# Block attention fused with two feed-forward layers: attention's small products in four quarters of the TensorE array, and the first block begun in another order

## The chip, the cores and the metric

One core of one Trainium2 chip runs the whole kernel. The metric is the device time of one execution in microseconds (us); lower is better. The kernel before took 1273.2 us (median of three runs).

## What is computed

Attention within chunks of 64 tokens (8 batches, 8 heads, 576 tokens, head size 64), then two feed-forward layers over the 4608 tokens of width 512. All data are float32.

```
scores = scale * q_c @ k_c^T ; scores -= max(scores) ; attn = exp(scores)
attn = attn / (sum(attn) + 1e-9) ; out = attn @ v_c        # per chunk of 64 tokens and head
h = x @ w_in ; g = h * clip(h + 3, 0, 6) / 6 ; y = g @ w_out            # 512 -> 2048 -> 512
h = y @ w_in2 ; solu = h * softmax(h) ; ln = layernorm(solu) * g_ln ; out = ln @ w_out2   # 512 -> 1024 -> 512
```

## The kernel before, in words

**Units and blocks.** Attention is done in 36 units. A unit holds two chunks of 64 tokens for all 8 heads, one chunk on partitions 0 to 63 and the other on 64 to 127. Four units make a block of 512 tokens, and the first layer runs over nine blocks (`b` from 0). A block is 16 steps `f`: `moe_h(f)` is 12 matmuls of 128x512 (line 376), ScalarE and VectorE make the gate from its result (lines 382, 386) and split it in a rounded high part and a low rest (393, 396), and `moe_o(f)` is 12 matmuls into four accumulator banks (407). `moe_o` runs one step behind `moe_h`.

**Attention beside the blocks.** While block `b` is multiplied, the attention of block `b+1` is worked off in `slot(b, f)` (line 800), one unit per group of four steps. At the end of a group the slot issues the product with v of one unit (`attn_pv`, line 355) and then the scores of the next (`scores`, line 279). In the steps between come the exponentials, the normalisation (`attn_norm`) and a transpose of the probabilities: for the units that block 0 prepares, on TensorE (line 330) with two copies by ScalarE (333), for later ones on VectorE in 16 pieces (345). Block 0 also converts all weights of the first layer (`rescale`, `convert_signs`, `convert_words`, `split_w_*`), mostly on VectorE. Before block 0 the four units of the first block go through attention alone (lines 438 to 490).

**The two products before.** A head's product contracts 64 values for each of two chunks. Both chunks are done in one matmul with all 128 partitions: one operand is laid out block-diagonally (`kbd` for the keys, `pbd` for the probabilities), with zeros written once (`diagonal`, line 95), so that chunk 0 uses columns 0 to 63 and chunk 1 columns 64 to 127. A head's 64 output rows go to partitions 0 to 63 or 64 to 127 by the head's parity. A unit therefore has 8 such matmuls for the scores and 8 with v.

**Order.** The schedule is manual: each engine executes its instructions in the order in which the code issues them. SyncE (SP) starts all DMAs. PSUM has eight banks: two `att` tiles in turn (line 91), two `h` banks in turn, four accumulators. In the first block the scores borrow the accumulators and the products with v the `h` banks.

Of the kernel before, what the change touches and what calls it, by code (L numbers as in the profile page):

```python
# [16 lines left out]
P = 128  # L17
# [4 lines left out]
def tile_kernel(  # L22
# [62 lines left out]
    def wo_slot(f, dtype):  # L85
        return wap.tile([P, 2, DM], dtype, tag=f"wo{f}", name=f"wo{f}")
# [8 lines left out]
    def diagonal(t, eng):  # L95

        for c in range(2):
            eng.memset(t[c * D : (c + 1) * D, 1 - c], 0.0)
        return t

    def wide(tag, dtype=F32):
        return ap1.tile([P, 2, DM], dtype, tag=tag, name=tag)

    kbd = diagonal(wide("kbd").rearrange("p c (h k) -> p c h k", h=H), nc.vector)
    pbd = wide("pbd").rearrange("p c (h k) -> p c h k", h=H)
    q_t, k_t, v_t, p_t, exps, sums, raws = {}, {}, {}, {}, {}, {}, {}
# [141 lines left out]
    def convert(*keys):  # L248
        convert_signs(*keys)
        convert_words()  # L250
# [13 lines left out]
    def split_w(n=2, eng=None):  # L264
        split_w_hi(n)
        split_w_lo(eng or nc.gpsimd)

    def att_psum():
        return ps_att.tile([P, DM], F32, tag="att", name="att")

    def h_psum():
        return ps_h.tile([P, DM], F32, tag="h", name="hp")

    def scores(u, ps):
        qt, kt = q_t.pop(u), k_t.pop(u)
        sc = ps().rearrange("p (a c k) -> p a c k", a=NHP, c=2)
        for h in range(H):
            r0 = (h % 2) * D
            nc.tensor.matmul(  # L279
                sc[r0 : r0 + D, h // 2], qt[:, h], kt[:, :, h], start=True, stop=True  # L280
            )
        return sc.rearrange("p a c k -> p (a c) k")

    def attn_scores(u, ps=att_psum, pt=None):
        scv = scores(u, ps)
        mx = asp.tile([P, H], F32, tag="mx", name="mx")
        nc.vector.tensor_reduce(out=mx, in_=scv, axis=AX.X, op=ALU.max)
        pt = att_tile(ap2, "p") if pt is None else pt
        nc.vector.tensor_sub(  # L289
            out=pt, in0=scv, in1=mx[:, :, None].to_broadcast([P, H, D])  # L290
        )
        nc.scalar.activation(out=pt, in_=pt, func=AF.Exp, scale=0.125)  # L292
        p_t[u] = pt

    def attn_scores_act(u):
        sc = scores(u, att_psum)
        mx = asp.tile([P, H], F32, tag="mx", name="mx")
        nc.vector.tensor_reduce(out=mx, in_=sc, axis=AX.X, op=ALU.max)
        nc.vector.tensor_scalar_mul(out=mx, in0=mx, scalar1=-0.125)
        exps[u] = sc, mx  # L300

    def attn_exp_act(u, heads):
# [4 lines left out]
        for h in heads:  # L307
            nc.scalar.activation(
                out=p_t[u][:, h], in_=sc[:, h], func=AF.Exp, scale=0.125,
                bias=mx[:, h : h + 1], accum_out=sums[u][:, h : h + 1],  # L310
            )
# [13 lines left out]

    def attn_transpose(u, pb=pbd, ps=att_psum):
# [4 lines left out]
        tv = tp.rearrange("p a (h q) -> p (a h) q", h=2)  # L331
        for c in range(2):
            nc.scalar.copy(
                out=pb[c * D : (c + 1) * D, c], in_=tv[c * D : (c + 1) * D]
            )

    def attn_transpose_dve(u, quads):

        pv = p_t[u].rearrange("p (a c) (b k) -> p c b a k", a=NHP, b=2)
        pb = pbd.rearrange("p c (a h) (e q) -> p h c e a q", h=2, e=2)  # L340
        for s in quads:
            for c in range(2):
                for e in range(2):
                    o = c * D + e * 32
                    nc.vector.transpose(  # L345
                        out=pb[o : o + 32, s // 2, c, s % 2],
                        in_=pv[s * 32 : s * 32 + 32, c, e],
                    )

    def attn_pv(u, pb, x_hi, x_lo, ps=att_psum, lo=True):  # L350
        vt = v_t.pop(u)
        xps = ps().rearrange("p (a t) -> p a t", a=NHP)
        for h in range(H):
            r0 = (h % 2) * D
            nc.tensor.matmul(  # L355
                xps[r0 : r0 + D, h // 2], vt[:, h], pb[:, :, h], start=True, stop=True
            )
        o = (u % UPB) * P
        hi, lo_ = x_hi[:, :, o : o + P], x_lo[:, :, o : o + P]
        nc.scalar.copy(out=hi, in_=xps)  # L360
        los.append((lo_, xps, hi))
        if lo:
            attn_lo()
# [59 lines left out]

    kbs, qps = [kbd], []
    for i in range(3):
        kbs.append(wo_slot(NF - 1 - i, F32).rearrange("p c (h k) -> p c h k", h=H))
    for i in range(3, 6):
        qps.append(wo_slot(NF - 1 - i, F32).rearrange("p c (h k) -> p c h k", h=H))
    vs = wo_slot(NF - 7, F32).rearrange("p c (h k) -> p c h k", h=H)

    def acc_psum(i):
        return lambda: ps_acc.tile([P, DM], F32, tag=f"acc{i}", name=f"acc{i}")

# [16 lines left out]
    make_identity(nc, ident)  # L450
    diagonal(pbd, nc.gpsimd)
    nc.gpsimd.memset(three, 3.0)
    xs = new_x()
    attn_scores(0, acc_psum(0))
    attn_scores(1, acc_psum(1))
# [11 lines left out]
    attn_pv(0, pbd, *xs, h_psum, lo=False)  # L467
    load_v(4)
    fetch("o", 2)
    fetch("i", 4)  # L470
    convert(("i", 0))
    attn_transpose(2, kbs[2])
    attn_norm(3)
    attn_pv(1, kbs[1], *xs, h_psum, lo=False)
    load_v(5)
# [4 lines left out]
    attn_lo()  # L480
    attn_transpose(3, kbs[3])
    attn_lo()
    split_w(1, nc.vector)
    rescale("i", 1)
    attn_pv(2, kbs[2], *xs, h_psum, lo=False)
    rescale("o", 0)
    attn_lo()
    attn_pv(3, kbs[3], *xs, h_psum, lo=False)
    attn_lo()
    attn_scores_act(4)  # L490
    for f in range(5, NF):
# [4 lines left out]
        later(f + 2)  # L496
    convert(("i", 1))
    split_w_hi()
# [72 lines left out]
    def bank(p, tag):  # L571

        c_t[p, tag] = att_psum() if p == 0 else ps_2.tile([P, DM], F32, tag=tag, name=tag)
        return c_t[p, tag]

    def part(p, n):
# [217 lines left out]

    def start_scores(u):
        if u < NU:
            (attn_scores_act if u <= 2 * UPB else attn_scores)(u)
            load_qk(u + 1)

    def slot(b, f):  # L800
        ph = (f + 1) % 4
        u = (b + 1) * UPB + (f + 1) // 4
        if ph == 0:
            w = u - 1
            if w < NU:
                attn_pv(w, pbd, *xn[w // UPB])
                p_t.pop(w, None)
                load_v(w + 2)
            start_scores(u)
        elif u < NU:  # L810
# [281 lines left out]
```

## Time and profile before

| what | value |
|---|---|
| median of three runs | 1273.2 us (1272.98 to 1276.15) |
| the profiled execution: its own time | 1273.34 us |
| the profiled execution: span from first to last instruction | 1271.6 us |
| TensorE (PE) busy | 1244.4 us, 98% |
| TensorE's weight loads (PEld) busy | 1020.5 us, 80% |
| VectorE (DVE) busy | 883.5 us, 69% |
| ScalarE (ACT) busy | 596.8 us, 47% |
| GpSimd (POOL) busy | 262.5 us, 21% |

The page cuts the span in 40 slices of 31.8 us. TensorE is at 9 tenths or more in all but the first and the last. VectorE is at 9 tenths in slices two to four, at 5 to 6 in the blocks after them, and higher again in the second layer. The chain that ended last is TensorE for 85% of the span, VectorE for 9%. Line 355 is 3% of that chain and line 279 2%.

### The profile page before, as it was taken

Reading aid. Unit: us, or ns where it says so; the run is one execution under the profiler, and the core shown is the slowest. Engines: PE = TensorE matmul, PEld = TensorE weight load, DVE = VectorE, ACT = ScalarE, POOL = GpSimd, SP = SyncE. Lnnn points to the kernel's source line nnn. Section 1 sums busy time; section 2 is a strip of 40 time slices with the busy share of each in tenths; the row PEclk is TensorE's granted clock in tenths of the full one; section 3 lists DMA queues with packets and bytes.
Section 4 is the critical chain, followed back from the end, with each engine's and each line's share of the span. In section 5 each row is a group of like instructions: output and inputs, shape, how many; then the busy total and the mean of one; then the engine's idle time right before and its main releaser. Section 6 shows DMA issues by size and latency. Waiting matters only on the chain.

```text
span 1271.6 us, 17613 instructions
## 1 busy us (share of the span) xinstructions
PE 1244.4 (98%) x6260; PEld 1020.5 (80%) x6260; DVE 883.5 (69%) x1666; ACT 596.8 (47%) x1097; POOL 262.5 (21%) x369
## 2 busy tenths in 40 slices
PE   5999999999999999999999999999999999999998
PEld 4788888888888888888888888888777888888887
DVE  6999555556556556556656655499998788887784
ACT  4776322322322322322322322354688777777785
POOL 1000000000000000000000000001477676666764
PEclk9999999999999999999999999999999999999999
DMA  9901200200200200200200200352123232323311
GB/s 326 376 26 28 81 26 25 84 26 25 84 26 25 84 26 26 84 25 25 84 26 25 83 26 1 116 166 68 55 62 100 68 97 72 95 70 95 92 60 62
DMA packets 68392, 93.70 MB, mean 74 GB/s; under 512 B 10192, under 2 KB 39120, under 8 KB 68304
## 3 DMA queue, kind: packets, MB, share of 16 engines
q1 hardware_dynamic: 68304, 92.58, 22.5%
q8 instruction: 49, 0.80, 0.3%
q14 instruction: 39, 0.32, 0.1%
HBM read 62.92 MB, written 18.87 MB: 64 GB/s over the span
## 4 chain that ended last, share of the span: by engine, by line
PE 85%; DVE 9%; ACT 2%; issue 2%; POOL 1%; SPq 1%; DMA 1%; DVEq 0%; POOLq 0%; ACTq 0%
PE acc L407 28%; PE hp L376 28%; PE po L751 14%; PE b L560 4%; PE c L560 3%; PE att L355 3%; PE a L560 3%; PE att L279 2%; DVE s L181 2%; DVE t L386 1%; DVE g_lo L396 1%; ACT g_hi L393 1%; DVE s L173 1%; DVE wo L638 0%; SPq L666 0%
## 5 line engine op out<-in xcount | busy, mean ns | idle before, releaser
L376 PE MATMUL hp<-x_hi,wi 128*128 128x512 f32 x1152 | 286.3, 390 | 4.0 <-ACT wi L255 2.6
L407 PE MATMUL acc<-g_hi,wo 128*128 128x512 f32 x1152 | 289.5, 393 | 0.6 <-ACT g_hi L393 0.6
L382 ACT ACTIVATE t<-hp,three 128x512 f32<-128x512 f32 x144 | 99.0, 688 | 377.5 <-PE hp L376 377.2
L376 PEld LDWEIGHTS hp<-x_hi,wi 128*128 128x128 f32 x1152 | 215.8, 188 | 50.1 <-ACT wi L255 3.4
L407 PEld LDWEIGHTS acc<-g_hi,wo 128*128 128x128 f32 x1152 | 214.0, 188 | 50.1 <-issue 5.3
L386 DVE SCALAR_TENSOR_TENSOR t<-t,hp 128x512 f32<-128x512 f32 x144 | 98.9, 687 | 205.3 <-ACT t L382 205.0
L77 POOL TENSOR_TENSOR wi<-s,wi 128x512 fp32r<-128x512 f32 x5 | 7.6, 1512 | 874.4 <-ACT wi L76 861.9
L396 DVE TENSOR_TENSOR g_lo<-t,g_hi 128x512 fp32r<-128x512 f32 x144 | 99.6, 692 | 82.9 <-ACT g_hi L393 82.3
L376 PE MATMUL hp<-x_lo,wi 128*128 128x512 f32 x576 | 154.8, 391 | 0.0
L407 PE MATMUL acc<-g_lo,wo 128*128 128x512 f32 x576 | 154.1, 389 | 0.0
L751 PE MATMUL po<-wi,wo 128*128 128x512 f32 x648 | 151.0, 389 | 1.0 <-ACT ob L760 1.0
L393 ACT CAST g_hi<-t 128x512 fp32r<-128x512 f32 x144 | 89.3, 620 | 118.8 <-DVE t L386 118.8
L751 PEld LDWEIGHTS po<-wi,wo 128*128 128x128 f32 x648 | 121.5, 188 | 26.8 <-ACT ob L760 1.4
L345 DVE STREAM_TRANSPOSE pbd<-p 32x128 f32<-32x128 f32 x448 | 135.6, 303 | 5.7
L376 PEld LDWEIGHTS hp<-x_lo,wi 128*128 128x128 f32 x576 | 108.7, 189 | 22.8
L407 PEld LDWEIGHTS acc<-g_lo,wo 128*128 128x128 f32 x576 | 108.1, 188 | 22.8
L666 ACT COPY wo<-wo 32x256 f32<-32x256 f32 x228 | 92.0, 404 | 16.8 <-DVE wo L648 10.2
L541 POOL TENSOR_TENSOR x_lo<-xr,x_hi 128x768 fp32r<-128x768 f32 (+1 forms) x32 | 70.0, 2208 | 70.5 <-ACT x_hi L534 70.5
L638 DVE SCALAR_TENSOR_TENSOR wo<-wo,r,wo 128x1024 f32<-128x1024 f32 x36 | 75.3, 2092 | 1.3
L735 POOL TENSOR_TENSOR wo<-wo,wo 128x1024 fp32r<-128x1024 f32 x26 | 65.0, 2499 | 6.8 <-issue 2.5
L292 ACT ACTIVATE p<-p 128x512 f32<-128x512 f32 x29 | 18.3, 632 | 67.8 <-DVE p L289 67.8
L630 ACT ACTIVATE wo<-wo,nmx 128x1024 f32<-128x1024 f32 x36 | 41.5, 1153 | 18.1 <-DVE nmx L627 17.9
(204 smaller groups left out, 1570.1 us busy)
## 6 DMA issues: line engine op xcount, KB each, us to landing
wi<-in_moe_w_in SPq DMA_DIRECT2D x24, 512.0 KB, 7.5
wo<-wo SPq DMA_DIRECT2D x328, 32.0 KB, 1.8
wo<-in_moe_w_out SPq DMA_DIRECT2D x19, 512.0 KB, 8.2
x2d<-xo SPq DMA_DIRECT2D x36, 256.0 KB, 2.9
out<-ob SPq DMA_DIRECT2D x36, 256.0 KB, 2.3
v<-in_v SPq DMA_DIRECT2D x34, 256.0 KB, 2.7
xr<-x2d SPq DMA_DIRECT2D x34, 256.0 KB, 3.2
q<-in_q SPq DMA_DIRECT2D x33, 256.0 KB, 3.5
```

The lines of the kernel that those rows point to most:

```text
L345: nc.vector.transpose(out=pb[o : o + 32, s // 2, c, s % 2], in_=pv[s * 32 : s * 32 + 32, c, e],)
L376: nc.tensor.matmul(hp, wi[f][:, a, kk * P : (kk + 1) * P], b[:, kk], start=(n == 0), stop=(n == 3 * KD - 1),)
L382: nc.scalar.activation(out=t, in_=hp, func=AF.Relu, bias=three[:])
L386: nc.vector.scalar_tensor_tensor(out=t, in0=t, scalar=6.0, in1=hp, op0=ALU.min, op1=ALU.mult)
L393: nc.scalar.copy(out=g_hi, in_=t)
L396: eng.tensor_sub(out=g_lo, in0=t, in1=g_hi.bitcast(F32))
L407: nc.tensor.matmul(acc[dc], wo[f][:, w, dc * P : (dc + 1) * P], g[i], start=(f == 0 and n == 0), stop=(f == NF - 1 and n == 2),)
L541: eng.tensor_sub(out=lo[:, f], in0=r, in1=hi[:, f].bitcast(F32))
L560: nc.tensor.matmul(ps, x[:, AT[a], j], w2[w, j][i], start=(start and n == 0), stop=(stop and n == 5), skip_group_check=True,)
L638: nc.vector.scalar_tensor_tensor(out=h, in0=e, scalar=r, in1=h, op0=ALU.mult, op1=ALU.mult, accum_out=mu)
L666: move(out=m[b * 32 : b * 32 + 32, a], in_=tr[a * 32 : a * 32 + 32, b])
L751: nc.tensor.matmul(po, a[f], wi[KD * NS + f][:, w], start=(n == 0), stop=(n == 3 * NF2 - 1),)
```

## The change

The operands are no longer block-diagonal. Each head and chunk is a matmul of its own, with 64 partitions and 64 columns, on one of four quarters of the array: the row half is the chunk `c`, the column half (the output partitions) the head's parity `e`. A unit's product is 16 such matmuls. The two chunks write to different PSUM banks, so an `att` tile has two banks and there is one of it; it holds the scores of one unit in the first half of each bank and the product with v of the unit before in the second half, and the slot issues the scores first. Keys and probabilities take half the room and get two buffers each (`u % 2`). A key tile is one DMA in place of two, the copy after a TensorE transpose one in place of two, the zero fills are gone. The TensorE transposes write to an `h` bank. The accumulators are two tiles of two banks. In the first block the order is rewritten, and the normalisations of units 1 and 3 go from VectorE to GpSimd. `maxima` reads the two banks; the exponentials index them by chunk.

```diff
-    ps_att = es.enter_context(tc.tile_pool(name="ps_att", bufs=2, space=PSUM))
+    ps_att = es.enter_context(tc.tile_pool(name="ps_att", bufs=1, space=PSUM))
...
-        k_t[u] = kbd if kt is None else kt
+        k_t[u] = ks[:, u % 2] if kt is None else kt
         nc.sync.dma_start(out=q_t[u], in_=q[u])
-        for c in range(2):
-            nc.sync.dma_start(
-                out=k_t[u][c * D : (c + 1) * D, c], in_=k[u, c * D : (c + 1) * D]
-            )
+        nc.sync.dma_start(out=k_t[u], in_=k[u])
...
+    def quarters(o, lhs, rhs):
+        for a in range(NHP):
+            for c in range(2):
+                for e in range(2):
+                    r = slice(c * D, (c + 1) * D)
+                    nc.tensor.matmul(
+                        o[e * D : (e + 1) * D, c, a], lhs[r, 2 * a + e], rhs[r, 2 * a + e],
+                        start=True, stop=True,
+                    )
...
-        tp = ps().rearrange("p (a t) -> p a t", a=NHP)
+        tp = h_psum().rearrange("p (a t) -> p a t", a=NHP)
         for a in range(NHP):
             nc.tensor.transpose(tp[:, a], pt[:, a], ident)
-        for c in range(2):
-            nc.scalar.copy(
-                out=pb[c * D : (c + 1) * D, c], in_=tv[c * D : (c + 1) * D]
-            )
+        pb = pts[:, u % 2] if pb is None else pb
+        nc.scalar.copy(out=pb, in_=tp.rearrange("p a (e q) -> p (a e) q", e=2))
...
-            for dc in range(KD):
-                acc[dc] = ps_acc.tile([P, BT], F32, tag=f"acc{dc}", name=f"acc{dc}")
+            for i in range(KD // 2):
+                acc[2 * i], acc[2 * i + 1] = pair_of(acc_psum(i))
...
-    load_qk(1, qps[0][:, 0], diagonal(kbs[1], nc.gpsimd))
-    load_qk(2, qps[1][:, 0], diagonal(kbs[2], nc.vector))
-    load_qk(3, qps[2][:, 0], diagonal(kbs[3], nc.gpsimd))
+    for u in range(1, UPB):
+        load_qk(u, qps[u - 1][:, 0], kbs[u - 1][:, 0])
     load_v(0)
+    fetch("i", 0)
     load_v(1)
-    fetch("i", 0)
...
-    attn_scores(2, acc_psum(2), qps[0][:, 1])
-    attn_transpose(0, pbd)
-    attn_norm(1)
-    attn_scores(3, acc_psum(3), qps[1][:, 1])
-    attn_transpose(1, kbs[1])
+    attn_scores(2, scores(2, att_psum()), qps[0][:, 1])
+    attn_norm(1, nc.gpsimd)
+    attn_scores(3, scores(3, acc_psum(0)), qps[1][:, 1])
+    attn_transpose(0)
     rescale("i", 0)
     attn_norm(2, nc.gpsimd)
...
         if ph == 0:
             w = u - 1
             if w < NU:
-                attn_pv(w, pbd, *xn[w // UPB])
+                t = att_psum()
+                if u < NU:
+                    sc = scores(u, t)
+                attn_pv(w, t, *xn[w // UPB])
```

How the instructions move is shown at three places; `_` and a number behind a name is the buffer. First TensorE in block 0, around the first transpose and the first slot (f = 2 and 3), before:

```order
L330 MATMUL att<-ident,p 128x128 x4
L376 MATMUL hp<-x_hi,wi_445 128x512 x8
L376 MATMUL hp<-x_lo,wi_445 128x512 x4
L355 MATMUL att<-pbd,v 64x128 x8
L279 MATMUL att<-kbd,q 64x128 x8
L407 MATMUL acc_490<-g_hi,wo_488 128x512
```

and in the changed kernel, where line 345 is the transpose, 385 `moe_h`, 416 `moe_o`, and 283 both products:

```order
L345 MATMUL hp<-ident,p 128x128 x4
L385 MATMUL hp<-x_hi,wi_497 128x512 x8
L385 MATMUL hp<-x_lo,wi_497 128x512 x4
L283 MATMUL att<-kbd,q 64x64 x16
L283 MATMUL att<-pbd,v 64x64 x16
L416 MATMUL acc_542<-g_hi,wo_540 128x512 x2
```

The transpose now takes an `h` bank between two of `moe_h`, the scores stand ahead of the product with v, and each is 16 matmuls of 64x64 in place of 8 of 64x128. Second, TensorE from the start of the program to the fourth product with v, before:

```order
L279 MATMUL acc_155<-kbd,q 64x128 x8
L279 MATMUL acc_169<-wo_106,wo_109 64x128 x8
L279 MATMUL acc_196<-wo_107,wo_110 64x128 x8
L330 MATMUL att<-ident,p 128x128 x4
L279 MATMUL acc_221<-wo_108,wo_111 64x128 x8
L330 MATMUL att<-ident,p 128x128 x4
L355 MATMUL hp<-pbd,v 64x128 x8
L330 MATMUL att<-ident,wo_109 128x128 x4
L355 MATMUL hp<-wo_106,v 64x128 x8
L330 MATMUL att<-ident,wo_110 128x128 x4
L355 MATMUL hp<-wo_107,wo_112 64x128 x8
L355 MATMUL hp<-wo_108,wo_112 64x128 x8
```

and now:

```order
L283 MATMUL acc_141<-kbd,q 64x64 x16
L283 MATMUL acc_163<-wo_104,wo_107 64x64 x16
L283 MATMUL att<-wo_105,wo_108 64x64 x16
L283 MATMUL acc_223<-wo_106,wo_109 64x64 x16
L345 MATMUL hp<-ident,p 128x128 x8
L283 MATMUL acc_262<-pbd,v 64x64 x16
L283 MATMUL att<-pbd,v 64x64 x16
L345 MATMUL hp<-ident,wo_107 128x128 x4
L283 MATMUL acc_333<-wo_104,wo_110 64x64 x16
L345 MATMUL hp<-ident,wo_108 128x128 x4
L283 MATMUL acc_360<-wo_105,wo_110 64x64 x16
L283 MATMUL att<-kbd,q 64x64 x16
```

All four scores now stand ahead of the first transpose. Third, ScalarE over the same stretch, before (292 exponential, 333 copy of a transpose, 164 rescaling of a raw weight, 360 high part of x, 255 high part of a weight):

```order
L292 ACTIVATE p<-p 128x512 x2
L292 ACTIVATE wo_109<-wo_109 128x512
L333 COPY pbd<-att 64x512 x2
L292 ACTIVATE wo_110<-wo_110 128x512
L333 COPY wo_106<-att 64x512 x2
L164 ACTIVATE wi_136<-wi_136 128x512
L360 CAST x_hi<-hp 128x4x128
L333 COPY wo_107<-att 64x512 x2
L360 CAST x_hi<-hp 128x4x128
L333 COPY wo_108<-att 64x512 x2
L255 CAST wi_267<-s 128x512
L164 ACTIVATE wi_140<-wi_140 128x512
```

and now, where 307, 347, 158, 369 and 249 are these lines:

```order
L307 ACTIVATE p<-p 128x512 x2
L307 ACTIVATE wo_107<-wo_107 128x512
L307 ACTIVATE wo_108<-wo_108 128x512
L347 COPY pbd<-hp 128x512
L158 ACTIVATE wi_122<-wi_122 128x512
L347 COPY pbd<-hp 128x512
L369 CAST x_hi<-acc_262 128x2x4x64
L369 CAST x_hi<-att 128x2x4x64
L347 COPY wo_104<-hp 128x512
L249 CAST wi_290<-s 128x512
L369 CAST x_hi<-acc_333 128x2x4x64
L158 ACTIVATE wi_128<-wi_128 128x512
```

Eight copies of half a tile became four of a whole one, and the first rescaling stands behind one copy in place of two pairs.

## Rows read from the trace of the kernel before

**Rows 1.** The page's busy times: us, share of the span, instructions.
```profile
PE 1244.4 (98%) x6260; PEld 1020.5 (80%) x6260; DVE 883.5 (69%) x1666; ACT 596.8 (47%) x1097; POOL 262.5 (21%) x369
```
**Rows 2.** The chain that ended last, around 390 us: start, us, what.
```profile
389.26 1.13 PE att L355 x15
390.39 0.87 PE att L279 x14
391.26 2.96 PE acc L407 x12
394.23 2.72 PE hp L376 x12
```
**Rows 3.** Timeline of one product's start, in narrow windows, then of the whole product.
```profile
19.38 0.13 PEld L355 LDWEIGHTS hp<-wo,v 128*64 128x64 f32 x1 [0.17 <-issue]
19.38 0.14 PEld L355 LDWEIGHTS hp<-wo,v 128*64 128x64 f32 x2 [0.17 <-issue]
...
19.38 0.33 PE L355 MATMUL hp<-wo,v 128*64 128x128 f32 x2
19.38 0.43 PE L355 MATMUL hp<-wo,v 128*64 128x128 f32 x3
...
19.38 1.09 PE L355 MATMUL hp<-wo,v 128*64 128x128 f32 x16
```
**Rows 4.** Windows: length; busy PE, PEld, DVE, ACT, POOL; clock, DMA share, GB/s.
```profile
48.40:72.80 24.40, 24.40 (x136) 20.08 (x133) 24.30 (x47) 18.09 (x44) 0.00 (x0) 1.00 0.57 226
...
97.20:121.60 24.40, 24.40 (x135) 20.07 (x133) 24.17 (x47) 17.39 (x42) 0.00 (x0) 1.00 0.11 34
...
391.20:415.20 24.00, 24.00 (x130) 19.77 (x129) 13.83 (x31) 6.35 (x11) 0.00 (x0) 1.00 0.12 33
```
**Rows 5.** Timeline in block 0, step 6: the gate, and the next moe_h.
```profile
71.93 0.68 DVE L386 SCALAR_TENSOR_TENSOR t<-t,hp 128x512 f32<-128x512 f32 x1
...
72.77 0.72 PE L376 MATMUL hp<-x_hi,wi 128*128 128x512 f32 x2
```
**Rows 6.** Timeline of the first 28 us, single rows.
```profile
1.19 1.20 SPq L118 DMA_DIRECT2D kbd<-in_k  x2
...
5.48 1.97 PE L279 MATMUL acc<-kbd,q 128*64 128x128 f32 x16 [5.48 <-DMA kbd<-in_k]
...
7.49 0.69 DVE L287 TENSOR_REDUCE mx<-acc 128x8 f32<-128x512 f32 x1 [4.19 <-PE acc L279]
...
11.01 0.68 DVE L319 TENSOR_REDUCE sm<-p 128x8 f32<-128x512 f32 x1
...
11.92 0.20 DVE L321 RECIPROCAL sm<-sm 128x8 f32<-128x8 f32 x1
...
12.28 1.04 POOL L322 TENSOR_TENSOR p<-p,sm 128x512 f32<-128x512 f32 x1 [7.50 <-DVE sm L321]
...
13.44 0.63 ACT L292 ACTIVATE wo<-wo 128x512 f32<-128x512 f32 x1 [1.69 <-DVE wo L289]
...
17.21 1.19 ACT L333 COPY wo<-att 64x512 f32<-64x512 f32 x2
...
18.42 0.69 ACT L164 ACTIVATE wi<-wi 128x512 f32<-128x512 f32 x1
...
19.14 0.43 DVE L173 TENSOR_SCALAR s<-wi 128x512 int32<-128x512 int32 x1 [1.58 <-ACT wi L164]
...
19.59 1.42 DVE L181 SCALAR_TENSOR_TENSOR s<-wi,s 128x512 int32<-128x512 int32 x2
...
27.10 0.58 ACT L360 CAST x_hi<-hp 128x512 fp32r<-128x512 f32 x1
```
**Rows 7.** Timeline of TensorE in the first slot of block 1.
```profile
149.33 0.98 PE L355 MATMUL att<-pbd,v 128*64 128x128 f32 x13 [0.51 <-DVE pbd L345]
```
**Rows 8.** Timeline at the end of block 0: the accumulators emptied and written again.
```profile
134.94 1.28 DVE L420 TENSOR_SCALAR xo<-acc 128x512 f32<-128x512 f32 x2
...
137.41 0.39 PE L407 MATMUL acc<-g_hi,wo 128*128 128x512 f32 x1
```

More of the change, by code (lines that the diff above doesn't have):

```diff
@@ L268, in att_psum, with acc_psum, part_of, scores @@
     def att_psum():
-        return ps_att.tile([P, DM], F32, tag="att", name="att")
+        return ps_att.tile([P, 2, DM], F32, tag="att", name="att")
+    def acc_psum(i):
+        return ps_acc.tile([P, 2, DM], F32, tag=f"acc{i}", name=f"acc{i}")
     def h_psum():
         return ps_h.tile([P, DM], F32, tag="h", name="hp")
[L274 to L280, printed above, removed]
-            )
-        return sc.rearrange("p a c k -> p (a c) k")
-    def attn_scores(u, ps=att_psum, pt=None):
-        scv = scores(u, ps)
-        mx = asp.tile([P, H], F32, tag="mx", name="mx")
-        nc.vector.tensor_reduce(out=mx, in_=scv, axis=AX.X, op=ALU.max)
+    def part_of(t, n):
+        w = DM // 2
+        return t[:, :, n * w : (n + 1) * w].rearrange("p c (a k) -> p c a k", a=NHP)
+    def quarters(o, lhs, rhs):
[7 more added lines that the diff above has]
+                    )
+    def scores(u, t):
+        sc = part_of(t, 0)
+        quarters(sc, q_t.pop(u), k_t.pop(u))
+        return sc
+    def maxima(sc):
+        mx = asp.tile([P, H], F32, tag="mx", name="mx")
+        nc.vector.tensor_reduce(
+            out=mx.rearrange("p (c a) -> p c a", c=2), in_=sc, axis=AX.X, op=ALU.max
+        )
+        return mx
+    def attn_scores(u, sc, pt=None):
+        mx = maxima(sc).rearrange("p (c a) -> p c a", c=2)
         pt = att_tile(ap2, "p") if pt is None else pt
         nc.vector.tensor_sub(
-            out=pt, in0=scv, in1=mx[:, :, None].to_broadcast([P, H, D])
+            out=pt.rearrange("p (a c) k -> p c a k", c=2), in0=sc,
+            in1=mx[:, :, :, None].to_broadcast([P, 2, NHP, D]),
         )
@@ L293, in attn_scores, with attn_scores_act, attn_exp_act @@
         p_t[u] = pt
[L295 to L298, printed above, removed]
+    def attn_scores_act(u, sc):
+        mx = maxima(sc)
         nc.vector.tensor_scalar_mul(out=mx, in0=mx, scalar1=-0.125)
         exps[u] = sc, mx
-    def attn_exp_act(u, heads):
+    def attn_exp_act(u, hs):
         sc, mx = exps[u]
@@ L306, in attn_exp_act @@
             sums[u] = asp.tile([P, H], F32, tag="sm", name="sm")
-        for h in heads:
+        for h in hs:
+            a, c = h // 2, h % 2
+            m = c * NHP + a
             nc.scalar.activation(
-                out=p_t[u][:, h], in_=sc[:, h], func=AF.Exp, scale=0.125,
-                bias=mx[:, h : h + 1], accum_out=sums[u][:, h : h + 1],
+                out=p_t[u][:, h], in_=sc[:, c, a], func=AF.Exp, scale=0.125,
+                bias=mx[:, m : m + 1], accum_out=sums[u][:, h : h + 1],
             )
@@ L345, in attn_transpose_dve, with attn_pv @@
                     nc.vector.transpose(
-                        out=pb[o : o + 32, s // 2, c, s % 2],
+                        out=pb[o : o + 32, s // 2, s % 2],
                         in_=pv[s * 32 : s * 32 + 32, c, e],
                     )
[L350 to L357, printed above, removed]
-        o = (u % UPB) * P
-        hi, lo_ = x_hi[:, :, o : o + P], x_lo[:, :, o : o + P]
-        nc.scalar.copy(out=hi, in_=xps)
-        los.append((lo_, xps, hi))
+    def attn_pv(u, t, x_hi, x_lo, pb=None, lo=True):
+        pv = part_of(t, 1)
+        quarters(pv, v_t.pop(u), pts[:, u % 2] if pb is None else pb)
+        o = (u % UPB) * P
+        hi, lo_ = (
+            x[:, :, o : o + P].rearrange("p a (c q) -> p c a q", c=2) for x in (x_hi, x_lo)
+        )
+        nc.scalar.copy(out=hi, in_=pv)
+        los.append((lo_, pv, hi))
         if lo:
@@ L421, in moe_o @@
                 nc.sync.dma_start(out=x2d[b, :, dc], in_=xo)
[L424 to L432, printed above, removed]
+    kbs, qps = (
+        [heads(wo_slot(NF - 1 - i, F32)) for i in r] for r in (range(3), range(3, 6))
+    )
+    vs = heads(wo_slot(NF - 7, F32))
     def later(f):
@@ L480, in tile_kernel @@
     attn_lo()
[L481 removed]
+    split_w(1, nc.vector)
+    attn_pv(2, acc_psum(0), *xs, kbs[0][:, 1], lo=False)
     attn_lo()
[L483 removed]
     rescale("i", 1)
[L485 removed]
+    attn_transpose(3, kbs[1][:, 1])
+    attn_lo()
+    attn_pv(3, acc_psum(1), *xs, kbs[1][:, 1], lo=False)
     rescale("o", 0)
+    convert_signs(("i", 1))
     attn_lo()
[L488 to L490 removed]
+    attn_scores_act(4, scores(4, att_psum()))
     for f in range(5, NF):
@@ L571, in bank @@
     def bank(p, tag):
-        c_t[p, tag] = att_psum() if p == 0 else ps_2.tile([P, DM], F32, tag=tag, name=tag)
+        if p:
+            c_t[p, tag] = ps_2.tile([P, DM], F32, tag=tag, name=tag)
+        else:
+            if not early:
+                early.append(att_psum())
+            c_t[p, tag] = early[0][:, int(tag == "b")]
         return c_t[p, tag]
+    early = []
     def part(p, n):
```

39 lines of the change are left out of this document (16 added, 23 removed).

## The prediction

> **What bounds the kernel now.** I read the busy times first: TensorE is busy 98% of the span and no other engine over 69% [rows 1]. Then the chain that ended last, in a block after the first: from slot to slot it holds nothing but matmuls [rows 2]. A group of four steps is eight runs of 12 matmuls at 2.72 us, 21.76 us, in a group of 24.00 us [rows 2, 4]; the slot with the two attention products is the remaining 2.24 us. That agrees with the chain: 1.13 and 0.87 for the products and 0.24 by which the first run after them is longer (2.96 against 2.72) [rows 2]. In these blocks VectorE is busy 13.83 of 24.00 us and ScalarE 6.35 [rows 4], so each microsecond taken from TensorE there is taken from the time. Block 0 is different: VectorE, which converts weights, is busy 24.30 of 24.40 us in the first of its groups and 24.17 in the third, beside a TensorE that is just as full [rows 4]. There are two bounds there at once. Before 28 us TensorE mostly waits, and the order of VectorE and ScalarE sets when the first `moe_h` can start.
>
> **One product, looked at closely.** A product of 8 heads is 16 matmul passes [rows 3], two for each head. Its first two weight loads lie together within 0.14 us, where one alone takes 0.13; two passes are over within 0.33 us, and the third ends 0.10 us behind them [rows 3]. So the two column halves of the array run side by side, and each half takes its passes in turn. The whole product is 1.09 us [rows 3], which is the 0.33 us of the first pair and seven more pairs at 0.109 us. Per slot this is 16 steps of 0.109 us, 1.74 us; the other 0.50 us of the 2.24 is getting in and out.
>
> **The slots.** The change makes 16 matmuls of 8, so 32 passes, each over 64 moving columns in place of 128. If all four quarters run side by side, a product is eight steps as before. How long a step then is, no row shows. The upper bound is 0.109 us again, no gain; the lower is half, 0.0545 us, since the columns halve. I take the half: a load and its pass alternate on each half now with no more than the pass itself between steps [rows 3]. A slot gains 16 x 0.0545 = 0.87 us. The product with v now follows the scores and has up to three waits, on v and on the transposed pieces, among its first four matmuls; for these I take 0.05 us off. That leaves **0.82 us a slot**. There are 32 slots, for units 4 to 35. The first three are in the part where VectorE is full, the last has no scores (0.41 us), and 28 are left: 23.0 + 0.4 us. That the slot now issues the scores first costs nothing: VectorE, which reads both, has ten idle microseconds in a group.
>
> **The first three slots.** There VectorE leaves 0.10 us a group free, 0.23 in the third [rows 4], and gets no work less. What is late next has a place: the transpose takes an `h` bank, so the `moe_h` behind it needs the bank of the one before, which VectorE frees with its gate. In step 6 the gate ended at 72.61 us and the next `moe_h` began at 72.77 [rows 5]. If TensorE comes 0.82 us earlier and VectorE does not, this wait eats all but 0.16 us. Bounds: 0.4 us for the three slots together (VectorE's free time) and 2.5 us (3 x 0.82); I take **0.8 us**, near the lower end, because VectorE is lighter only from the third group on.
>
> **The start.** The key tile is one DMA: of the 1.20 us that its two issues took, about 0.6 goes, and the first product, which waited for the second of them until 5.48 us, begins at about 4.9. It took 1.97 us there, against 1.09 later [rows 3, 6]; with half the columns I allow 1.2, so the first maximum starts at 6.1 in place of 7.49 [rows 6]. From there I lay the new order end to end. VectorE: four maxima and four subtractions at 0.70, two sums with reciprocal at 1.11 (from 11.01 to 12.12) [rows 6]: 7.8 us, 13.9. ScalarE: exponential 0.63, one copy 0.6 (half of the 1.19 for two), rescaling 0.69 [rows 6]: 15.8. VectorE: 0.43 and 1.42 for the words of the first weight, then the sum of unit 3, 1.11 [rows 6]: 18.8. GpSimd normalises in 1.04 [rows 6]: 19.9. Transpose, copy, product and cast at some 0.6 us each: 22.4. Before, this last cast ended at 27.68 [rows 6]. That is 5.3 us; of it 1.4 comes from the earlier first maximum, 1.4 from two normalisations that leave VectorE, 2.4 from four copies less on ScalarE, and these overlap in part. Two normalisations of 1.04 us on GpSimd replace 0.7 on VectorE; they are in the chain once, for unit 3. I take **4.5 us**, with bounds of 2.5 (the DMA brings nothing and TensorE, now more idle, is as slow per pass as in its first product) and 5.5. The order behind it is the same VectorE work, so the lead lasts.
>
> **Small edits.** The first slot of block 1 waited 0.51 us for the transposed probabilities [rows 7]; with the scores ahead, **0.4 us** of it goes (0 to 0.7). Accumulators in pairs must be emptied in pairs before they are written: VectorE's two copies ended at 136.22 us and the next write began at 137.41 [rows 8], so 1.2 us cover it; without that cover it would cost up to 0.7 us eight times. The single `att` tile is written again a whole group, some 23 us, after its readers. The zero fills ran before 5.48 us, while TensorE waited for keys, and are worth nothing. Strided reads over two banks have the same 512 elements a partition: nothing, hidden by VectorE's idle time after block 0. The second layer is not touched.
>
> **The sum.** 23.0 + 0.4 + 0.8 + 4.5 + 0.4 = 29.1 us. The profiled execution's own time was 1273.34 us, 0.1 above the median of the runs, so the forecast is **1244.3 us**. From the bounds: at worst 0.70 a slot, 0.4, 2.5 and 0, which is 22.9 us (1250.5); at best 0.87, 2.5, 5.5 and 0.7, which is 33.5 us (1239.9).
>
> **Rivals.** *Half of a pass is fixed.* If half of the 0.109 us does not shrink with the columns, a pass is 0.082 us, a slot gains 0.38, and the sum is 10.6 + 0.2 + 0.6 + 4.5 + 0.4 = 16.3 us: 1257.0. For it: only one width of pass is in the rows. Against: passes follow each other without a gap on each half [rows 3]. Chance 0.07. The Trainium skill, "TensorEngine Tiling (Array Packing)", section Performance Considerations, speaks against the change in this way: it states about 60 cycles of overhead a matmul and warns against taking the tiling from a dimension that is already small. By that, as an estimate, 25 ns would stand on top of 0.0545, a slot would gain 0.42 and the time would be about 1256 us. No run here shows a 64-column pass yet.
>
> *Two at a time.* The trace shows column halves side by side, never row halves. The code issues both passes of a quarter together, and the second must wait for the first; if no more than two quarters are ever fed past such a wait, a product is 16 steps of 0.0545 us, which is 0.87 us as before, and the slots gain nothing. Only the start and the wait in block 1 remain: 1273.3 - 4.9 = 1268.4. For it: nothing past two is seen. Against: the second load starts within 0.01 us of the first, past the first head's waiting second pass [rows 3], and the same step should reach the third quarter. Chance 0.09.
>
> *Slower: the weight loads take turns.* The change doubles the loads of a product from 16 to 32, each still of 64 columns. If loads of the two row halves exclude one another, 32 loads need 32 x 0.0545 = 1.74 us where the passes need 0.44. Its place is every product, its price 0.87 us for 63 of them in the slots, 54.8 us, less 2.5 at the start: 1325.6. It decides from the point at which loads come more than about 0.027 us apart, for then the gain is gone. Against it: two loads in 0.14 us [rows 3], and the row halves read different partitions. Chance 0.06. That the change does not do what it says is excluded by the order: 16 matmuls of 64x64 stand there.
>
> **How the numbers follow.** Four quarters with half steps: 0.78. The range 1239 to 1257 us holds that case's bounds with 0.9 us below, and reaches up to the case of the half-fixed pass; that leaves out the other two, 0.15, and some tail. A measurement of this kernel tells about 0.3%, 3.8 us, from no change. Faster by more: the first two cases and most of two at a time, 0.90; within: 0.04; slower: 0.06.
>
> **What would show it.** Right: product lines with 512 weight loads and passes become 1024 of 64x64, with some 0.6 us from the first load to the last end of a product; groups of 23.2 us in the blocks after the first; the first `moe_h` at 22.5 to 24 us in place of 27.7; in block 0 groups near 24.3 us with TensorE waiting for the gate. Wrong: groups of 24.0 us or more after block 0, weight loads of one product spaced by 0.05 us, or a `moe_h` in later blocks that waits for an `h` bank.

## The result, and the profile after

The changed kernel took 1251.74 us (median of four runs, 1247.80 to 1252.34), the kernel before 1273.09 us beside it: a ratio of 0.9815 with a 95% interval of 0.9803 to 0.9827, 21.4 us less. Three of the four runs took 1251.43 to 1252.34 us at mean granted clocks of 0.990 to 0.993, the fourth 1247.80 at 0.997; what sets that one apart is not known. The profiled execution took 1251.43 us, its span is 1249.6 us. In the changed kernel line 283 is both attention products, 345 the transpose, 385 `moe_h`, 416 `moe_o`, 563 the products of the second layer and 602 one of its sums on VectorE (`sum_2`).

The busy times, which answer to [rows 1]: TensorE fell by 24.8 us and its weight loads by 22.3, the other engines by 4 us at most.

```profile
PE 1219.6 (98%) x7412; PEld 998.2 (80%) x7412; DVE 883.6 (71%) x1660; ACT 592.9 (47%) x1089; POOL 260.3 (21%) x365
```

**A slot.** The chain that ended last, in the stretch that answers to [rows 2] (start, us, what):

```profile
347.98 2.72 PE hp L385 x12
350.70 1.09 PE att L283 x64
351.79 2.95 PE acc L416 x12
354.74 2.72 PE hp L385 x12
```

Both products are now one piece of 1.09 us, and the run behind it is 0.23 longer than 2.72. A slot is 1.32 us where it was 2.24 [rows 2]. TensorE's timeline of that slot, matmuls and then weight loads (start, us, engine, line, operation, tile, shape, count), answers to [rows 3]:

```profile
350.63 0.69 PE L283 MATMUL att<-kbd,q 64*64 64x64 f32 x32
351.15 0.65 PE L283 MATMUL att<-pbd,v 64*64 64x64 f32 x32
```
```profile
350.63 0.56 PEld L283 LDWEIGHTS att<-kbd,q 64*64 64x64 f32 x32 [0.35 <-issue]
351.09 0.56 PEld L283 LDWEIGHTS att<-pbd,v 64*64 64x64 f32 x32
```

32 passes fit in 0.69 us. The single records say how: the first four weight loads start at 350.631, 350.638, 350.645 and 350.651, the next four 0.055 us later, and so on; the last four begin 0.870 us after the first four, 15 steps of 0.058 us. All four quarters are fed side by side, two of the same row half no worse than two of different ones.

**Windows.** Two windows of 23.50 us in block 0 and one group of a later block, which answer to [rows 4]:

```profile
43.00:66.50 23.50, 23.50 (x166) 19.27 (x165) 23.46 (x44) 17.12 (x42) 0.00 (x0) 1.00 0.63 253
66.50:90.00 23.50, 23.21 (x162) 18.67 (x161) 23.40 (x46) 16.77 (x42) 0.00 (x0) 1.00 0.11 34
...
350.70:373.78 23.08, 23.08 (x165) 18.97 (x166) 13.84 (x32) 6.35 (x10) 0.00 (x0) 1.00 0.12 36
```

A later group is 23.08 us in place of 24.00. In block 0 VectorE still has next to no free time (23.46 and 23.40 of 23.50), and TensorE now has a little (23.21 of 23.50).

**The waits of TensorE**, from 40 us on (what waited, on what; total us, times, longest):

```profile
PE att L563 <- DVE u L602: 6.3, 1, 6.3
PE b L563 <- DVE u L602: 2.0, 1, 2.0
...
PE hp L345 <- DVE p L337: 0.7, 2, 0.4
...
PE att L283 <- DVE pbd L357: 0.2, 1, 0.2
```

The first row is new and by far the largest. The second stood in the kernel before too, at the same 2.0 us. The lead over the kernel before, read at three points (the store of block 0's, block 7's and block 8's first result), grows from 5.8 us (134.83 to 129.04) to 31.3 us (806.77 to 775.49), and falls to 23.1 us (900.97 to 877.91): **block 8 gives 8.2 us back**. At the end of the span it is 22.0 us (1271.6 to 1249.6). TensorE's timeline in block 8:

```profile
849.59 2.07 PE L563 MATMUL att<-wi,x_hi 128*128 128x512 f32 x4 [6.31 <-DVE u L602]
851.46 1.05 PE L563 MATMUL att<-wi,x_lo 128*128 128x512 f32 x2
852.32 2.71 PE L385 MATMUL hp<-x_hi,wi 128*128 128x512 f32 x8
```
```profile
848.87 0.67 DVE L602 TENSOR_TENSOR u<-s,att 128x512 f32<-128x512 f32 x1
```

and the windows from 847.00 on (the 0.50 is the granted clock):

```profile
847.00:853.80 6.80, 4.21 (x10) 3.34 (x11) 2.54 (x5) 0.59 (x1) 0.00 (x0) 0.50 0.00 0
853.80:860.00 6.20, 6.20 (x28) 5.12 (x28) 2.55 (x5) 2.39 (x4) 0.73 (x1) 1.00 0.00 0
```

The waiting matmuls are `product_2` of the first pair in the second layer. The change gave its two early accumulators, `a` and `b`, the two banks of one `att` tile (`early[0][:, int(tag == "b")]`), where the kernel before had two tiles. `product_2` writes bank `a`; `sum_2`, on VectorE, reads bank `b`. `sum_2` stands behind weight conversion on VectorE's queue and runs at 848.87. TensorE stood for 6.31 us up to 849.59; from 847.0 to 853.8 the granted clock was 0.50 (1.2 GHz), and four matmuls took 2.07 us that elsewhere take 1.07.

**The start.** Rows of the timeline up to the first `moe_h`, which answer to [rows 6]:

```profile
4.23 1.13 PE L283 MATMUL acc<-kbd,q 64*64 64x64 f32 x32 [4.23 <-DMA kbd<-in_k]
```
```profile
5.42 0.69 DVE L295 TENSOR_REDUCE mx<-acc 128x8 f32<-128x512 f32 x1 [5.42 <-PE acc L283]
...
8.31 0.69 DVE L295 TENSOR_REDUCE mx<-acc 128x8 f32<-128x512 f32 x1 [1.47 <-PE acc L283]
```
```profile
20.59 0.79 PE L345 MATMUL hp<-ident,wo 128*128 128x128 f32 x4 [0.92 <-POOL wo L337]
22.05 1.13 PE L283 MATMUL acc<-wo,wo 64*64 64x64 f32 x32 [0.68 <-ACT wo L347]
...
23.97 1.65 PE L385 MATMUL hp<-x_hi,wi 128*128 128x512 f32 x3
```

The first maximum starts at 5.42 in place of 7.49 and the first `moe_h` at 23.97 in place of 27.73 us, a lead of 3.8 us.

### The profile page after: what moved, and what is told of

Its sections match the earlier page's. It is cut to its first block, busy times and chain, and to the rows that moved or that the text cites. A ratio compares the mean times of both kernels' runs of the same rounds, so it can differ in the third digit from the quotient of the medians.

```text
span 1249.6 us, 19798 instructions
## 1 busy us (share of the span) xinstructions
PE 1219.6 (98%) x7412; PEld 998.2 (80%) x7412; DVE 883.6 (71%) x1660; ACT 592.9 (47%) x1089; POOL 260.3 (21%) x365
## 4 chain that ended last, share of the span: by engine, by line
PE 83%; DVE 11%; ACT 2%; issue 1%; SPq 1%; DMA 1%; POOL 1%; DVEq 0%; ACTq 0%
PE acc L416 27%; PE hp L385 27%; PE po L761 14%; PE b L563 5%; PE c L563 3%; PE a L563 3%; DVE s L175 3%; PE att L283 3%; SPq L676 1%; DVE g_lo L405 1%; DVE t L395 1%; DVE s L167 1%; PE att L563 1%; DVE wi L255 1%; DMA wo<-wo 1%
## 5 line engine op out<-in xcount | busy, mean ns | idle before, releaser
L648 DVE SCALAR_TENSOR_TENSOR wo<-wo,r,wo 128x1024 f32<-128x1024 f32 x36 | 78.3, 2175 | 1.3
```

Of the source, the lines that this page charges most:

```text
L648: nc.vector.scalar_tensor_tensor(out=h, in0=e, scalar=r, in1=h, op0=ALU.mult, op1=ALU.mult, accum_out=mu)
```

## The experiments

The theory after the result: the four quarters do what was forecast, the start too, and the missing 8 us is the wait of `product_2`, made by putting two banks into one tile. Each experiment is the changed kernel with one edit, unless it says otherwise. A ratio is to the kernel before as it ran beside that experiment: 1273.09 us beside the change, 1274.60 beside e1, e2, e3 and e6, 1274.66 beside e4, e7, e8 and e9, 1272.76 beside e10 and e11. Differences of 2 us between these groups are therefore not sure.

### e1: the two early banks as tiles of their own

```diff
-    ps_att = es.enter_context(tc.tile_pool(name="ps_att", bufs=1, space=PSUM))
...
+    es_att = ExitStack()
+    ps_att = es_att.enter_context(tc.tile_pool(name="ps_att", bufs=1, space=PSUM))
...
             if not early:
-                early.append(att_psum())
-            c_t[p, tag] = early[0][:, int(tag == "b")]
+                es_att.close()
+                early.append(es.enter_context(tc.tile_pool(name="ps_e", bufs=2, space=PSUM)))
+            c_t[p, tag] = early[0].tile([P, DM], F32, tag="e", name="e")
```

> The last step pairs of block 8 begin the second layer with two partial sums; in the changed kernel both live in one two-bank tile, here each has a tile of its own again, in the same two banks. Theory (a wait between two halves of one tile): the second product of unit pair 0 no longer waits 6.3 us for VectorE's sum, TensorE's clock does not fall there, and the time is 8 us lower, about 1243.5 us. Rival (VectorE is simply behind in block 8, whoever waits): the wait moves to the next product that needs VectorE, 4 us or more of it stays, and the time is 1248 to 1252 us.

Measured: 1244.41 us (1243.55 to 1244.93), ratio 0.9760 (0.9746 to 0.9775). Its timeline in block 8 has the product with no wait ahead of it, and the sum well behind it:

```profile
842.13 0.39 PE L564 MATMUL e<-p,x_lo 128*128 128x512 f32 x1
842.36 1.07 PE L564 MATMUL e<-wi,x_hi 128*128 128x512 f32 x4
```
```profile
848.12 0.67 DVE L604 TENSOR_TENSOR u<-s,e 128x512 f32<-128x512 f32 x1
```

The product starts 5.8 us before the sum for which it waited in the changed kernel, and the granted clock stays at 1.00.

From block 7's first store to block 8's it takes 94.00 us (774.73 to 868.73), the changed kernel 102.42, the kernel before 94.20. The same products write and read the same amounts; the tile that holds the banks differs, and the `att` pool now stands behind the accumulators'. So the wait followed the tile: the product never needed the sum. Right behind block 8 e1 has two waits of TensorE of 1.6 us each, up to 869.94 and 878.71 us, which the changed kernel and e2 don't have. Whether the moved pool makes them was not tried.

### e2: the same tile, the product issued later

```diff
-        12: (product_6, product_2),
-        13: (product_5, product_7, sums_7),
+        12: (product_6, sum_2),
+        13: (product_2, product_5, product_7, sums_7),
```

> The two-bank tile is kept, but the second product of unit pair 0 is issued one step later, behind 24 more matmuls (5.4 us). Theory: the 6.3 us wait is covered but for 1 us; the third product then waits about 1 us for ScalarE's copy out of the shared half; the time is 1244 to 1247 us. Rival (VectorE behind in any case): 1249 to 1252 us.

Measured: 1244.24 us (1243.05 to 1245.46), ratio 0.9760 (0.9745 to 0.9774). `product_2` waits 0.9 us for `sum_2` in place of 6.3, and another 1.1 us wait appears:

```profile
PE att L563 <- ACT wo L614: 1.1, 1, 1.1
...
PE att L563 <- DVE u L602: 0.9, 1, 0.9
```

Block 8 is 96.5 us here (774.88 to 871.39), 2.5 more than in e1, yet the whole time is the same within the measurement; 1.3 of the 2.5 come back behind block 8 (371.8 us to the end, in e1 373.1). The wait can be cured in the tile or in the order.

### e3, e7, e8, e10: the order of the 16 matmuls of a product

These leave every matmul as it is and change the order of the loops in `quarters`, from heads outermost (`a`, `c`, `e`), which visits all four quarters for each pair of heads. They ask how far ahead TensorE can go past a quarter that is busy. e3 does one row half and then the other:

```diff
-        for a in range(NHP):
-            for c in range(2):
+        for c in range(2):
+            for a in range(NHP):
```

> The 16 matmuls of a product are issued with all eight of one chunk first, so that the first eight use only the two quarters of one row half. If TensorE reaches less than eight matmuls ahead, only two quarters work at a time: a product is 16 steps of 0.058 us in place of 8, a slot is 0.9 us longer, groups after block 0 go back to 24.0 us, and the time is about 1280 us. If it reaches a whole product ahead, nothing changes: groups of 23.08 us and 1250 to 1252 us.

Measured: 1265.66 us (1263.48 to 1266.39), ratio 0.9925: neither end. From its chain:

```profile
356.85 1.50 PE att L283 x58
358.34 2.99 PE acc L416 x12
...
380.37 1.50 PE att L283 x58
```

A group is 23.52 us. The weight loads of the second row half begin 0.294 us after those of the first, 5 steps, though nothing of the first is needed. e7 goes quarter by quarter:

```diff
-        for a in range(NHP):
-            for c in range(2):
-                for e in range(2):
+        for c in range(2):
+            for e in range(2):
+                for a in range(NHP):
```

> The changed kernel with the 16 matmuls of a product issued quarter by quarter (four heads on one quarter, then the next). What e3 showed is a look-ahead: with pairs of quarters the second pair began 5 steps of 0.058 us after the first, the next product's pairs at 10 and 15. A queue that starts a pass at most six passes ahead of the oldest one not yet started gives just these three numbers. By that theory, worked out pass by pass, a slot's two products take 31 steps here against 16, so 15 x 0.058 = 0.87 us more a slot, over 32 slots 27.8 us: 1279.5, slot 2.2 us, and the second quarter begins two steps after the first. Rival one, no look-ahead past a quarter that is busy: 64 steps, 2.8 us more a slot, 1341. Rival two, a look-ahead that holds a whole product (e3 then was slow for another reason, the distance between the two row halves): 1252 to 1254.

Measured: 1304.94 us (1304.77 to 1305.21), ratio 1.0241: slower than the kernel before, and none of the three numbers.

```profile
351.01 2.62 PE att L283 x64
353.62 2.94 PE acc L416 x12
...
375.61 2.62 PE att L283 x64
```

A group is 24.60 us. The loads of the second quarter begin 0.288 us after the first, again five steps and not two, so the queue of six passes in common is wrong. Both orders have runs of eight passes on a quarter, and both let the next quarter in when the sixth of the eight starts. So it is a matter of each quarter: **passes are handed out in order, and behind the one that runs on a quarter two more can wait; a third holds up everything behind it.** Worked out pass by pass, this gives 16, 23 and 43 steps for a slot's two products in the change, e3 and e7. e8 cuts the runs to four passes on a pair of quarters:

```diff
-        for a in range(NHP):
-            for c in range(2):
-                for e in range(2):
+        for g in range(0, NHP, 2):
+            for c in range(2):
+                for a in (g, g + 1):
+                    for e in range(2):
```

> The changed kernel with the loops cut in two: for two pairs of heads the upper row half, then the lower, then the other two pairs, so eight passes of one row half stand together in place of 16 (e3) or 4 (the change). The queue of six passes gives 18 steps for the two products against 16 and 24: 0.12 us more a slot, 3.7 us in all, 1255.4; the second pair of quarters begins one step after the first. Rival, the loss of e3 goes with the count of passes that stand together (halfway between 4 and 16 on a line is a third of e3's loss of 14 us): 1256.4 with the second pair of quarters two or more steps late; or a queue as long as this run: 1251.7.

Measured: 1252.00 us (1250.99 to 1252.78), ratio 0.9825, no different from the change and below the 1255.4 of the queue of six; 17 steps by the queues of two. e10 was worked out with them before it ran: runs of four on one quarter after another (e8 with the loops over `e` and `a` exchanged).

> The changed kernel with runs of four passes on each quarter in turn (two heads on one quarter, the same two on the next). The theory of a common queue of six passes fell with e7, whose second quarter began at step 5 and not at 2. New theory: passes are handed out in order, and behind the pass that runs on a quarter two more can wait; a third holds up everything behind it. It gives 16, 23, 17 and 43 steps for a slot's two products in the change, e3, e8 and e7, as their weight loads show. For this order it gives 19: quarters begin at steps 0, 1, 2, 3 and then without a gap, so 3 x 0.058 = 0.17 us more a slot, over 32 slots 5.6 us: 1257.3. Rival, one pass can wait: 34 steps, 1285. Rival, three can wait: 16 steps, 1251.7.

Measured: 1255.96 us (1254.74 to 1256.61), ratio 0.9864. The chains of e8 and of e10:

```profile
351.20 1.14 PE att L284 x62
...
374.34 1.14 PE att L284 x62
```
```profile
351.10 1.23 PE att L284 x61
...
374.36 1.23 PE att L284 x61
```

A group is the distance of the two rows. All five together, with a step of 0.058 us:

| order | steps by the queues | more a group, worked out | measured group | more a group | time, us |
|---|---|---|---|---|---|
| the change | 16 | 0 | 23.08 | 0 | 1251.7 |
| e8 | 17 | 0.06 | 23.14 | 0.06 | 1252.0 |
| e10 | 19 | 0.17 | 23.26 | 0.18 | 1256.0 |
| e3 | 23 | 0.41 | 23.52 | 0.44 | 1265.7 |
| e7 | 43 | 1.57 | 24.60 | 1.52 | 1304.9 |

The groups agree within 0.05 us; for e10 the number stood before the run, with 1257.3 us for the kernel. One part of it did not come true. The quarters were to begin a step (0.058 us) apart, and the single records of e10 have them begin 0.013 us apart; in e8 the second pair of quarters begins 0.027 us after the first. From the second run on the rule fits: in e10 the second quarter's fifth pass starts 0.287 us after the first load, with the first quarter's sixth (0.286). So a slot's first four passes on a quarter go in without the hold-up, and why is open. Whether the two waiting places are weight loads, passes or both, these runs don't tell.

### e6 and e9: the start

e6 loads a key tile with two DMAs again, and the second v tile ahead of the first weights, as in the kernel before:

```diff
-        nc.sync.dma_start(out=k_t[u], in_=k[u])
+        for c in range(2):
+            nc.sync.dma_start(
+                out=k_t[u][c * D : (c + 1) * D], in_=k[u, c * D : (c + 1) * D]
+            )
...
     load_v(0)
+    load_v(1)
     fetch("i", 0)
-    load_v(1)
```

> Every key tile is loaded by two DMAs of 64 partitions again, and the second v tile is asked for ahead of the first weight, as in the kernel before; all else as changed. Theory (the earlier keys give part of the lead of the start): the first product starts about 0.6 us later than 4.2, the second some 1 us later than 7.1, the first moe_h 0.6 to 1.4 us later than 23.97, and the time is about 1 us higher. Rival (VectorE's and ScalarE's order alone sets the start): the first moe_h within 0.3 us of 23.97 and the time unchanged.

Measured: 1252.14 us (1250.38 to 1253.35), ratio 0.9825. The first maximum starts at 6.70 in place of 5.42 and the first `moe_h` at 25.16 in place of 23.97: the two edits together are worth 1.2 us at the start, and the time doesn't show it (0.4 us, less than the runs scatter).

e9 puts the start back into the order of the kernel before, with quarters and single key DMAs kept:

```diff
-    attn_norm(1, nc.gpsimd)
-    attn_scores(3, scores(3, acc_psum(0)), qps[1][:, 1])
     attn_transpose(0)
+    attn_norm(1)
+    attn_scores(3, scores(3, acc_psum(0)), qps[1][:, 1])
+    attn_transpose(1)
     rescale("i", 0)
     attn_norm(2, nc.gpsimd)
-    attn_transpose(1)
...
-    attn_norm(3, nc.gpsimd)
+    attn_transpose(2, kbs[0][:, 1])
+    attn_norm(3)
...
-    convert_words()
+    convert(("i", 1))
```

> The changed kernel (quarters, key tile in one transfer) with the first block begun in the order of the kernel before: units 1 and 3 normalised on VectorE, each transpose ahead of the next scores, the words of the second weight converted where they were. Theory: most of the start's gain is from the products and from having one copy in place of two, and the new order is worth the two normalisations that leave VectorE: the first moe_h comes at 24.7 to 25.5 us in place of 23.3 to 24.0, and the time is 1253 to 1253.5. Rival one: the order makes the lead; first moe_h at 26.5 to 27, time 1254.5 or more. Rival two: in block 0 VectorE is the bound, the order in front of it is hidden by then or even costs: time 1251 to 1252 whatever the first moe_h does.

Measured: 1253.77 us (1252.69 to 1254.04), ratio 0.9838 (0.9824 to 0.9853), 2.0 us more than the change, whose interval just overlaps. Its first `moe_h`:

```profile
24.88 1.42 PE L385 MATMUL hp<-x_hi,wi 128*128 128x512 f32 x5 [0.51 <-ACT x_hi L369]
```

The fair partner is e1, which has the start of the change and in which the second key tile was used as early as here (second maximum at 7.31, in e9 at 7.28; 8.31 in the changed kernel's profile). There it is

```profile
23.29 2.07 PE L386 MATMUL hp<-x_hi,wi 128*128 128x512 f32 x4
```

so the new order is worth 1.6 us at that point and 2.1 us at the first store (128.35 against 130.49); the other 2.9 us of e1's lead of 4.4 (27.73 to 23.29) come from the products, the copy and the DMA, which were not tried one by one. A faster TensorE does not make e1's lead: in these rows five matmuls take 1.42 us in e9 and four 2.07 in e1.

### e4 and e11: the old wait in the second layer

Two tries to gain more on top of e1, at the 2.0 us wait that both kernels have. e4 exchanged products 5 and 7 of the third pair:

```diff
-    product_7(2)
-    product_5(2)
+    product_5(2)
+    product_7(2)
```

> Built on e1 (the early banks apart), with one exchange in the second layer: product 5 of the third pair is issued ahead of product 7, which in e1 waits 1.96 us for the sum of that pair; this wait was in the kernel before too. Theory: the wait is plain time, and six matmuls at 0.23 us (1.36 us) now lie in it, so about 1.3 us less than e1, 1243.1. Rival: the sum or what reads the product late is needed at the same moment further on, and the wait moves there: 1244.4, as e1.

Measured: 1245.52 us (1244.68 to 1245.94), ratio 0.9774 (0.9760 to 0.9789), not below e1. The row of 2.0 us is still there: the wait is of another pair, so this edit tells nothing. e11 took the right pair:

```diff
-    soft_2(2)
     product_6(3)
     sum_2(3)
+    soft_2(2)
```

> Built on e1, in place of e4, which exchanged two products of a pair that did not wait: the wait of 1.96 us is that of product 7 of pair 3 for its sum, which VectorE does behind the second half of a softmax (4.5 us). Here product 6 and the sum stand ahead of that half. Theory: the 1.96 us are plain time, the sum is done before product 7 comes, 1242.5. Rival: what the softmax half feeds (the turn and the output product) comes some 0.7 us later and TensorE waits there: 1243.5 to 1244.4.

Measured: 1246.27 us (1245.09 to 1248.05), ratio 0.9788 (0.9773 to 0.9802), 1.9 us more than e1 and above both expected times. TensorE's waits in it, from 900 to 960 us:

```profile
PE po L763 <- ACT ob L772: 3.0, 1, 3.0
PE b L564 <- DVE u L623: 1.9, 1, 1.9
PE a L564 <- ACT s L595: 1.0, 1, 1.0
PE b L564 <- DVE u L604: 0.3, 1, 0.3
```

The 2.0 us became 0.3, and waits of 3.0 and 1.9 took its place, where e1 has 1.1 and none. In e1 VectorE is busy 37.0 of the 40 us from 900 on and ScalarE 32.8; in e11 the granted clock also fell there (mean 0.96 over these 40 us, 1.00 in e1). So taking one wait away moved it. That the two engines together bound this stretch is the likely reason, and is not shown.

**The best version** is e1 or e2: 1244.4 and 1244.2 us, 7.3 and 7.5 us below the change and 2.4% below the kernel before.

## Why the prediction was right, and where not

The forecast was 1244.3 us with a range of 1239 to 1257 and "faster" at 0.90. The measured 1251.7 lies in the range, 7.4 us above the forecast. It lies there only because the range was drawn up to the rival at 1257: the forecast's own bounds for the four quarters end at 1250.5.

- **"The second layer is not touched": this step failed.** The small edits were gone through for added work and for buffers that are written again, but not for what the merged `att` tile does to its second user; the new `early` tile is not among the edits told ahead of the prediction either. It cost 6.3 us of waiting and some 2 us more at the granted clock of 0.50 (4.2 us from 849.59 to 853.8 for half as much work), about the 8.2 us of block 8. The small edit that did get a place, the accumulators in pairs, cost nothing, as put: none of TensorE's waits from 40 us on names line 416. e1 takes only that away and lands on 1244.41. That this is the forecast to 0.1 us is luck. e1's lead is 6.5 us at block 0's first store (6.1 forecast), grows by 25.6 over blocks 1 to 7 (23.0 forecast) and by 0.2 in block 8, and falls by 2.4 behind it, where nothing was forecast; the last two errors cancel.
- **A slot: 0.82 us forecast, 0.92 measured.** The mechanism is as put: four quarters, half steps. The step is 0.058 us and not 0.0545, which costs 16 x 0.004 = 0.06; getting in and out shrank from 0.50 to 0.39 us; and the 0.05 taken off for waits at the product with v did not occur. So a slot gained more than the 0.87 us that the forecast had as its best case. Over blocks 1 to 7 the lead grew by 25.5 us (5.8 to 31.3) where 27 x 0.82 + 0.41 + 0.4 = 23.0 was forecast.
- **Block 0: right in size, wrong in what waits.** From the third `moe_h`, 4.3 us ahead of the kernel before, to the first store, 5.8 ahead, its four slots gave 1.5 us; 0.8 + 0.82 was forecast. VectorE does fill the first groups: from slot to slot (47.07, 71.33, 95.71 and 119.29 us) they are 24.26, 24.38 and 23.58 us, where the kernel before has 24.39, 24.38 and 24.39. So the first two slots brought 0.14 us together, and the third, from which VectorE is lighter, 0.81. But TensorE waits there for the normalised probabilities (the third row of the waits), not for an `h` bank that the gate frees.
- **The start: 4.5 us forecast, 3.8 in this profile**, and 4.4 in e1, where the second key tile arrived 1.0 us earlier. Keys arrived earlier than allowed for (the first maximum 5.42 against 6.1), and VectorE put some 2.1 us of weight conversion ahead of unit 3's sum (15.09 to 17.23 us in e1), as laid out. What was sized too small is TensorE behind it: in e1 unit 3's transpose and product take 1.11 and 1.13 us (from 19.59 and 21.38), 0.6 each was allowed; the lower bound had named a TensorE as slow as in its first product. The order's share is 1.6 us by e9.
- **The wait in block 1: 0.4 us forecast, 0.3 measured** (0.51 [rows 7] to 0.2).
- **The rival with a half-fixed pass fell**: its step of 0.082 us would show in the loads, which are 0.058 apart. The 1251.7 us lie near its 1257.0 only because of block 8. The Trainium skill, "TensorEngine Tiling (Array Packing)", section Performance Considerations, puts some 60 cycles on every matmul and advises against tiling a dimension that is already small. In this kernel's trace halving the columns from 128 to 64 took the step from 0.109 to 0.058 us, so no more than 0.004 us stood on top of the half; the trace does not bear the page out.
- **Two at a time fell** in the change as written: the third and fourth quarter start within 0.02 us of the first. But it was not far: with the same matmuls in another order, e7, mostly one or two quarters are at work at a time, and the kernel is slower than before.
- **The rival with turn-taking loads fell**: loads of different quarters start 0.007 us apart.

## What to carry to other kernels

When small matmuls share the array in quarters, issue them round the quarters, one matmul each; two each cost 0.18 us a group here (e10), four each 1.52 (e7), and the order alone moved the kernel from 1251.7 to 1304.9 us. When two buffers become halves of one tile, list every later user of that tile: a write to one half waited 6.3 us for a read of the other. And when a gain is read in one stage, read the lead at the end of every stage; block 8 stood out at once.

## What was not expected of the hardware

- Passes of different quarters overtake one another, over the border of two products. In e7's timeline a pass of the product with v starts ahead of passes of the scores that were issued before it:

```profile
352.09 0.27 PE L283 MATMUL att<-pbd,v 64*64 64x64 f32 x1
352.14 0.22 PE L283 MATMUL att<-kbd,q 64*64 64x64 f32 x1
```

The Trainium skill, "TensorE: Matmul & The Clock Gate", Part 3, The mechanism, says that matmuls start and end in program order. These rows don't agree, and the measurement decides: over the border of the two products the order did not hold, and the sentence ahead of the prediction that each engine executes in the order of the code is too strong for TensorE. The rows don't name the quarter, so that the order holds within one is taken from the model and not seen.

- The reach of that overtaking is short: two passes behind the running one on a quarter fit all five orders above, but for the first four passes on a quarter in a slot.
- The granted clock of the first windows must be read beside the durations. From 12 to 24 us it is 0.73 in the changed kernel and 1.00 in e1, for the same instructions, but the product with v of unit 2 takes 0.69 us in the changed kernel and 1.13 in e1:

```profile
12.00:24.00 12.00, 7.95 (x177) 6.25 (x177) 9.72 (x21) 7.53 (x14) 3.13 (x3) 0.73 1.04 415
```
```profile
12.00:24.00 12.00, 9.33 (x175) 7.39 (x175) 9.44 (x19) 7.26 (x13) 3.12 (x3) 1.00 1.03 415
```
```profile
18.98 0.69 PE L283 MATMUL acc<-wo,wo 64*64 64x64 f32 x32 [0.68 <-ACT wo L347]
```
```profile
18.43 1.13 PE L284 MATMUL acc<-wo,wo 64*64 64x64 f32 x32 [0.68 <-ACT wo L348]
```

In e1 all transposes and products of these 12 us take 1.08 to 1.13 us, as long as those of the changed kernel at 0.50 (1.11 from 14.32 us), and e1's first four `moe_h` matmuls take the 2.07 us of four at 0.50 in block 8. So TensorE ran at the lower level in e1 there, whatever the 1.00 says, and in the changed kernel at the upper level for a part. What made it rise sooner there was not tried.
